# Score search ahead of the slot sums in every pair, and query weights three heads ahead

## The chip, the cores and the metric

The kernel runs on one core of a Trainium2 chip. The metric is the device time of one execution in microseconds, as the median of several runs. Names of engines in the profile: PE is TensorE's matmul, PEld its weight load, DVE is VectorE, ACT is ScalarE, POOL is GpSimd, SP is SyncE, which issues most of the DMAs.

## The reference

A normalised input `xn` of 2048 tokens by 512 feeds two branches, and both are added to `x`.

```python
xn = layernorm(x)
# A: attention, 32 heads of 16, one shared key and value head
p = softmax(q @ k.T * 16 ** -0.5); A = (p @ v) @ wo
# B: product-key experts, 32 heads, 64 x 64 = 4096 experts
s1 = q1 @ k1.T; s2 = q2 @ k2.T          # per head, 64 scores each
# two best of each, four candidate sums, the best two of them are the experts of the head
g = softmax(top_s)
act = gelu(xn . u[top_e]); B = sum(g * act * v[top_e])
out = x + A + B
```

So each token has 64 slots (32 heads, two experts), each with a row of `u`, a row of `v`, a gate and a gelu.

## The kernel before, in words

The tokens are four groups of 512, called phases 0 to 3, each of four tiles of 128 tokens. Phases 0 and 1 take part of the experts' work slot by slot; phases 2 and 3 do it densely over all 4096 experts, by one-hot matrices of gates. The 32 heads are 8 blocks `c` of four. The order of the score stages is `SEQ`: phase 0 with all blocks, phase 1 with two, phase 2 with all and its dense stage, phase 1 with the other six, phase 3 with all and its dense stage.

Everything after the start stands in a schedule written out by hand: a loop over `d`, 256 pairs of attention steps and some more at the end. `att_steps` (L1136) issues in each pair: score matmuls of one key block (`sc`, L326) with their exponentials on ScalarE (`pt`, L329), the `pv` matmuls of the pair before (L340), then `mid()`, the score matmuls of the next key block, a projection block if one is due (L433), and `fill()`. Score tiles for the exponentials have two PSUM buffers, `pv` one, and everything else (`psc`, `pw`, `pwt`, `pwo`, `pact`, `pout` and so on) shares three PSUM buffers with tag `x`.

`fill()` (L1313) runs `score_thread` by costs until the spent cost reaches an aim that grows evenly over the pairs, at most 4.0 a pair. The thread yields pieces of expert scores (`psc`, L531, 12 matmuls a tile), the making of the next block's combined weights (`wp_make`: `pw`, L486, `pwt`, L493, and the split of a weight tile into a high and a low part, L495 on ScalarE and L496 on VectorE), and the dense stages. When a score tile is complete, `item` (L512) searches it on VectorE: eight MAX8 (L544) and eight FIND_INDEX8 (L546). The search is what releases the PSUM buffer. After the fourth tile of a block `batch` (L563) does the index arithmetic (L571 to L632); the gates follow two pairs later, after an exponential on ScalarE (L583), in `gates` (L605 or L634).

`mid()` (L1258) does the slot work on VectorE. In order: tanhs of finished groups of four slots (L998, on ScalarE), then `dots` (L982, the product of a gathered row of `u` and the token), the slot weights (`w`, L1005), and then `go()` (L1288): sums `xa += w * v` (L1017), interleaved with `CHAIN`, the gelu polynomials of groups just completed (`gq`, `gy`, `ga`, L991 to L993), and with `rest`, the work held in `BEHIND`: gates, low parts of splits, and the sums of projection blocks (L437). It ends with up to four gathers on POOL (L970), which wait for the sums to free one of twelve buffers, and with stores of finished rows (L449). A group's tanh is issued in the `mid()` of the pair after its polynomial.

`dense_on` says which stage runs: 0 score tiles, 4 the last two score tiles of a dense phase, 2 the one-hot stage, 3 its end, 1 the dense sums. In stage 2 alone `go` is put into `POST_FILL`, which `fill()` runs at its end, and there the polynomials are issued in `mid()` directly after the dots.

The dense thread starts with `spread` (L749, `ptd` at L752): it transposes three tables. The third needs the last gates; until `gated_all` is set the thread gives the pair back without more work.

Query weights are loaded by `wp_load` (L465), 512 KB a head, on SP's queue, two heads ahead in buffers of tag `gy` (three of them, also used for gates in the dense stage). Tag `wd` has four buffers, used from the one-hot stage on.

Of the kernel before, what the change touches and what calls it, by code (L numbers as in the profile page):

```python
# [11 lines left out]
F32 = mybir.dt.float32  # L12
# [11 lines left out]
P = 128  # L24
S = 2048
D = 512
# [7 lines left out]
NC = 8  # L34
# [21 lines left out]
def tile_kernel(ctx, tc, x, wq, wkv, wo, wqT, kT, uv, ub, vb, out):  # L56
# [5 lines left out]
    late = [None]  # L62
# [383 lines left out]
    def experts_out(t):  # L446
        acc, last = ACC[t], t // GT == QB[3]
        assert last or t in DONE_A
        store(lambda: nc.sync.dma_start(d_part[t] if last else out[t * P:(t + 1) * P, :], acc))  # L449
        LIVE.discard(t)  # L450
# [14 lines left out]
    def wp_load(c, h):  # L465
        if late[0] is None or (c == 1 and h < 2):
            w = gtile(F32, (P, 2, D), "wqt") if c == 0 and h > 1 else big.tile([P, 2, D], F32, name="wqt", tag="wqt", bufs=2)
        else:
            w = late[0].tile([P, 2, D], F32, name="wqt", tag="gy", bufs=3)
        nc.sync.dma_start(w, wqT[4 * c + h].rearrange("(s p) d -> p s d", p=P))  # L470
        WC["raw", c, h] = w

    def wk_tile():
        return big.tile([P, 2, 512], F32R, name="wk", tag="wk", bufs=NWK)

    def wp_make(c):

        wt = [big.tile([P, 2, 512], F32, name="wt", tag="da", bufs=2) for _ in range(2)]
        for h in range(4):
            for n in range(4 * c + h + 1, min(4 * c + h + 3, 4 * NC) if late[0] else 4):  # L480
                if ("raw", n // 4, n % 4) not in WC:
                    wp_load(n // 4, n % 4)
            w = WC.pop(("raw", c, h))
            p = xtile("pw")
            for s in range(2):
                nc.tensor.matmul(p[s * E:(s + 1) * E, :], kTs[:, s, :], w[:, s, :], start=True, stop=True)  # L486
            nc.scalar.copy(wt[h // 2][:, h % 2, :], p)
            yield 0.9
        WC[c] = []
        for k in range(KC):  # L490
            p = xtile("pwt")
            for h in range(4):
                nc.tensor.transpose(p[:, h * P:(h + 1) * P], wt[h // 2][:, h % 2, k * P:(k + 1) * P], ident)  # L493
            wk = wk_tile()
            nc.scalar.copy(wk[:, 0, :], p)  # L495
            nc.vector.tensor_tensor(out=wk[:, 1, :], in0=p, in1=wk[:, 0, :], op=OP.subtract)  # L496
            WC[c].append(wk)
            store(lambda k=k, wk=wk: nc.sync.dma_start(d_w[c][:, k], raw(wk[:])))
            yield 0.45
# [501 lines left out]
    def weigh(n):  # L1001
        if n not in WT and n < a_ready[0] // SB:
            ga, th = GA.pop(n), TH.pop(n)
            w = small.tile([P, SB], F32, name="w", bufs=3)
            nc.vector.scalar_tensor_tensor(w, th, 1.0, ga, op0=OP.add, op1=OP.mult)  # L1005
            WT[n] = w
# [17 lines left out]
    def gathers(most):  # L1024
        while g_next[0] < NSL and g_next[0] < a_next[0] + NGB - lent[0] and most > 0:
            gather(g_next[0])
            g_next[0] += 1
            most -= 1

    def dots(to):  # L1030
        while d_next[0] < min(to, NSL):
            dot(d_next[0])
            d_next[0] += 1

    def adds(most):
        while a_next[0] < a_ready[0] and most > 0:
            add(a_next[0])
            a_next[0] += 1
            most -= 1

    def tanhs(to):
        while a_ready[0] + SB <= to:
            tanh(a_ready[0] // SB)
            a_ready[0] += SB
# [8 lines left out]
    def run(fns):  # L1053
        todo = fns[:]
        fns.clear()
        for fn in todo:
            fn()
# [6 lines left out]
    def flush():  # L1064
        posts()
        for _ in range(2):
            for fns in (ON_ACT, LAST, LATER, BEHIND):
                run(fns)
            ON_ACT.extend(LATER_ACT)
            LATER_ACT.clear()  # L1070
        run(ON_ACT)
        run(BEHIND)
# [40 lines left out]
    dense_on, quiet = [0], [0]  # L1113
# [3 lines left out]
    def run_scores(until=None, key=None):  # L1117
        while (until is not None and spent[0] < until) or (key is not None and key not in IDX):
            posts()
            try:  # L1120
                cost = next(sgen)
            except StopIteration:
                spent[0] = 1e9
                posts()
                return
            if cost is None:

                if key is None:
                    return
                continue  # L1130
            spent[0] += cost

    STEPS = 512


    def att_steps(d, mid, fill):  # L1136
        i = 2 * d
        run(STORES)
# [11 lines left out]
        if 0 < i <= STEPS:  # L1150
# [3 lines left out]
            if pk == 14:  # L1154
                unit_tail(pu)
        mid()
        if i < STEPS:
            scores(u, kc + 1, 0)
# [36 lines left out]
    for h in range(4):  # L1195
        wp_load(0, h)
# [8 lines left out]
    for i in range(2):  # L1205
        for k in range(2):
            w = start.tile([P, 2, 512], F32R, name="wqs", tag="wqs", bufs=4)
# [26 lines left out]
    run(STORES)  # L1234
    start_stack.close()
    wp_load(1, 0)
    wp_load(1, 1)
    late[0] = pool("late", bufs=1)
# [3 lines left out]
    with tc.manual_schedule(engines={E_.PE, E_.Activation, E_.DVE, E_.Pool, E_.SP}):  # L1242
        done0 = spent[0]
        half = STEPS // 2
        pos, since = 0.0, half
        for d in range(half + 24):


            if dense_on[0] != 0:
                since = d  # L1250
            if dense_on[0] == 1:
                pos += 2.6 if d < half * 3 // 4 else max(0.0, NSL - pos) / max(half - 3 - d, 1)
            else:
                pos += (2.1 if len(IDX) < NC * TPH else 2.3 if 0 <= d - since < 12 else 1.75, 0, 1.4, 1.5, 0.5)[dense_on[0]]

            todo = max(min(int(pos + 0.001), g_next[0]) - d_next[0], 0)

            def mid():  # L1258
                post = POST[:]
                POST.clear()  # L1260
                for act, _ in post:
                    act()
                tanhs(d_next[0])
                run(ON_ACT)
                ON_ACT.extend(LATER_ACT)
                LATER_ACT.clear()
                run(LAST)
                LAST.extend(LATER)
                LATER.clear()
                rest = BEHIND[:]  # L1270
                BEHIND.clear()

                dots(d_next[0] + todo - 1)
                if a_ready[0] > a_next[0]:
                    weigh(a_next[0] // SB)
                dots(d_next[0] + 1 if todo > 0 else 0)
                for _, fn in post:
                    fn()
                sums = min(a_ready[0] - a_next[0], max(todo, 3) if d < half else 4)
                if dense_on[0] > 2:  # L1280
                    sums = min(sums, 2)
                if quiet[0] > 0:
                    quiet[0] -= 1
                    sums = 0
                if dense_on[0] == 2:
                    run(CHAIN)

                def go():  # L1288
                    n = sums
                    while rest or CHAIN or n > 0:  # L1290
                        if n > 0:
                            adds(1)
                            n -= 1
                        elif not rest:
                            run(CHAIN)
                        if CHAIN:
                            CHAIN.pop(0)()
                        if rest:
                            rest.pop(0)()
                    gathers(4)  # L1300

                    for _ in range(1 if d < half - 4 else NT):
                        if OUTS:
                            experts_out(OUTS.pop(0))

                if dense_on[0] == 2:
                    POST_FILL.append(go)
                else:
                    go()

            aim = done0 + (FILL - done0) * (d + 1) / half if d < half else 1e6

            def fill():  # L1313
                run_scores(until=min(aim, spent[0] + MOST))
                run(POST_FILL)

            att_steps(d, mid, fill)
        flush()
        run(STORES)
        while a_next[0] < NSL:  # L1320
            dots(NSL)
            run(CHAIN)
            tanhs(d_next[0])
            adds(SB)
            run(STORES)
            gathers(NGB)
        assert not OUTS
        run(STORES)
# [37 lines left out]
```

## Time and profile before

| | |
|---|---|
| median of 3 runs | 1946.3 us (1936.64 to 1952.67) |
| profiled execution | 1941.6 us, span 1939.9 us |
| mean granted TensorE clock | 0.98 |
| score stages of phases 0, 1, 2 | about 145 to 611 us of the span |
| one-hot and dense stage of phase 2 | about 611 to 1085 us |
| the other score stages | about 1090 to 1437 us |
| one-hot and dense stage of phase 3 | about 1437 to 1908 us |

A row of the waits names who waited, its line, who ended the wait, the total, how often, and the longest. A row in order of time has start, length, engine, line, operation, tiles and count, and in brackets the idle time of the engine just before it and what ended it. "Busy" of PE counts pipelined matmuls with modelled ends.

### The profile page before, as it was taken

The numbers are of one execution on the slowest core, as the hardware profiler recorded it, in microseconds if no ns is written. First come the engines' busy times: TensorE is split into PE (matmuls) and PEld (weight loads), VectorE is DVE, ScalarE is ACT, GpSimd is POOL, SyncE is SP. The second block draws the span as 40 slices with busy tenths as digits, with TensorE's granted clock in tenths as the row PEclk, the third lists the DMA queues.
The fourth block names the chain that finished last, engine by engine and source line by source line (L and its number), as shares of the span: only waits on it lengthen the run. The fifth ranks groups of instructions, "written<-read, shape, count | busy, mean of one in ns | idle before, by whom it ended". The sixth has DMA issues, their size and how long they took to land.

```text
span 1939.9 us, 34783 instructions
## 1 busy us (share of the span) xinstructions
PE 1867.8 (96%) x10990; PEld 994.5 (51%) x10990; DVE 1674.6 (86%) x6717; ACT 1294.0 (67%) x1803; POOL 561.4 (29%) x536
## 2 busy tenths in 40 slices
PE   6879999999999999999999999999999999999998
PEld 4634444555554544555555445555555445555553
DVE  6627788999999986999999889999998779999994
ACT  3336666655556887777877555555578877788873
POOL 1202223222221222343444332222212124344430
PEclk9979999999998999999999999999998999999999
DMA  7857889787773667899899978877646788989882
GB/s 271 309 186 250 281 271 300 274 297 259 245 242 100 210 224 254 247 284 295 267 286 304 361 272 274 275 232 268 213 130 200 239 239 279 287 271 293 279 274 85
DMA packets 234393, 491.11 MB, mean 253 GB/s; under 512 B 93396, under 2 KB 93396, under 8 KB 234204
## 3 DMA queue, kind: packets, MB, share of 16 engines
q0 software_dynamic: 73728, 268.47, 41.8%
q1 hardware_dynamic: 159240, 219.56, 34.8%
q8 instruction: 88, 1.44, 0.3%
q10 hardware_dynamic: 1236, 0.82, 0.1%
q14 instruction: 101, 0.83, 0.1%
HBM read 427.41 MB, written 56.07 MB: 249 GB/s over the span
## 4 chain that ended last, share of the span: by engine, by line
PE 65%; DVE 21%; DMA 3%; ACT 2%; issue 2%; SPq 0%; ACTq 0%; DVEq 0%
PE pv L340 18%; PE sc L326 13%; PE psc L531 10%; PE pact L727 9%; PE pout L855 9%; DVE i L546 5%; DVE xa L1017 3%; DVE m L544 3%; DVE g L982 3%; PE pwo L433 2%; PE pg L809 2%; ACT pt L329 2%; PE pw L486 2%; DVE oh L777 1%; DMA rw<-in_ub_dram 1%
## 5 line engine op out<-in xcount | busy, mean ns | idle before, releaser
L329 ACT ACTIVATE pt<-sc 128x1024 f32<-128x1024 f32 x1024 | 993.4, 1026 | 453.5 <-PE sc L326 404.7
L970 POOL DMA_INDIRECT g<-in_uv_dram,idx x512 | 553.5, 1081 | 1324.5 <-DVE xa L1017 673.3
L340 PE MATMUL pv<-pt,vaug 128*32 128x512 f32 x4096 | 509.4, 615 | 0.0
L326 PE MATMUL sc<-qa,kaug 64*128 64x512 f32 x2048 | 387.7, 453 | 12.3 <-ACT pt L329 11.3
L531 PE MATMUL psc<-wk,xt 128*128 128x512 f32 x1536 | 388.6, 400 | 7.4 <-DVE wk L496 3.5
L1017 DVE SCALAR_TENSOR_TENSOR xa<-g,w,xa 128x512 f32<-128x512 f32 x512 | 372.2, 745 | 0.1
L982 DVE CUSTOM_DVE_ANT_0 g<-g,xa 128x512 f32<-128x512 f32 x512 | 335.5, 681 | 11.9 <-DMA g<-in_uv_dram,idx 11.9
L531 PEld LDWEIGHTS psc<-wk,xt 128*128 128x128 f32 x1536 | 277.6, 188 | 111.4 <-issue 40.2
L326 PEld LDWEIGHTS sc<-qa,kaug 64*128 64x128 f32 x2048 | 157.1, 186 | 334.2 <-ACT pt L329 206.0
L340 PEld LDWEIGHTS pv<-pt,vaug 128*32 128x32 f32 x4096 | 108.8, 111 | 253.7 <-issue 252.0
L546 DVE FIND_INDEX8 i<-m,psc 128x8 uint32<-128x64 f32 x1024 | 206.4, 221 | 0.0
L727 PE MATMUL pact<-xt,wk 128*128 128x512 f32 x768 | 197.5, 402 | 1.1 <-DVE i L546 1.1
L855 PE MATMUL pout<-wk,wd 128*128 128x512 f32 x768 | 194.9, 402 | 0.2 <-DVE wd L913 0.2
L727 PEld LDWEIGHTS pact<-xt,wk 128*128 128x128 f32 x768 | 140.1, 189 | 50.8 <-issue 18.2
L855 PEld LDWEIGHTS pout<-wk,wd 128*128 128x128 f32 x768 | 140.8, 188 | 47.4 <-DVE act L982 5.1
L544 DVE MAX8 m<-psc 128x8 f32<-128x64 f32 x1024 | 146.0, 214 | 19.3 <-PE psc L531 18.6
L692 DVE TENSOR_TENSOR wk<-rw,wk 128x512 fp32r<-128x512 f32 x128 | 84.8, 683 | 12.9 <-ACT wk L691 12.9
L858 DVE TENSOR_TENSOR da<-da,pout 128x512 f32<-128x512 f32 x128 | 82.7, 679 | 9.7 <-PE pout L855 9.6
L691 ACT CAST wk<-rw 128x512 fp32r<-128x512 f32 x128 | 73.9, 628 | 6.4 <-DMA rw<-in_ub_dram 6.4
L777 DVE TENSOR_TENSOR oh<-oh 128x2048 f16<-128x2048 f16 x64 | 78.0, 1219 | 0.0
L809 PEld LDWEIGHTS <-oh 128*128 128x128 f16 x1024 | 68.5, 163 | 14.5 <-issue 8.8
L809 PE MATMUL pg<-oh 128*128 128x32 f16 x1024 | 73.6, 247 | 1.9 <-DVE oh L780 1.9
(156 smaller groups left out, 1285.9 us busy)
## 6 DMA issues: line engine op xcount, KB each, us to landing
wk<-dw SPq DMA_DIRECT2D x96, 512.0 KB
wqt<-in_wqT_dram SPq DMA_DIRECT2D x32, 512.0 KB
dw<-wk SPq DMA_DIRECT2D x32, 512.0 KB
rw<-in_ub_dram SPq DMA_DIRECT2D x64, 256.0 KB
rw<-in_vb_dram SPq DMA_DIRECT2D x64, 256.0 KB
gy<-dg SPq DMA_DIRECT2D x64, 256.0 KB
qa<-dqh SPq DMA_DIRECT2D x128, 64.0 KB
g<-in_uv_dram,idx POOLq DMA_INDIRECT x512
```

The source lines that it names most:

```text
L326: nc.tensor.matmul(p[:, b, :], kaug[o:o + 64, kc * P:(kc + 1) * P], QA[u][o:o + 64, i, :], start=True, stop=True)
L329: nc.scalar.activation(pt, p, AF.Exp, scale=SCALE)
L340: nc.tensor.matmul(PV[u][32 * j:32 * j + 32, :], vaug[:, kc, :], pt[:, b, :], start=kc == 0, stop=kc == 15)
L531: nc.tensor.matmul(p, XT[g][k][:, a, j * P:(j + 1) * P], WC[n_][k][:, bb, :], start=n == 0, stop=n == 11)
L544: nc.vector.max(m8[:, jb, s, :], p[:, s * E:(s + 1) * E])
L546: nc.vector.max_index(i8[:, jb, s, :], m8[:, jb, s, :], p[:, s * E:(s + 1) * E])
L727: nc.tensor.matmul(p, us[:, a, k * P:(k + 1) * P], XT[DG][k][:, c, :], start=n == 0, stop=n == 11)
L809: nc.tensor.matmul(p[:, i * NB:(i + 1) * NB], oa[:, :, i], ob[:, :, i], start=True, stop=True)
L855: nc.tensor.matmul(p, wd[0][:, a, j * P:(j + 1) * P], vs[:, c, :], start=n == 0, stop=n == 5)
L970: nc.gpsimd.indirect_dma_start(out=gt, out_offset=None, in_=uv, in_offset=bass.IndirectOffsetOnAxis(ap=IDX[ph, c, ti][:, s:s + 1], axis=0))
L982: nc.vector.tensor_tensor_reduce(u, u, XN[TPH * ph + ti], scale=1.0, scalar=0.0, op0=OP.mult, op1=OP.add, accum_out=a[:, i:i + 1])
L1017: nc.vector.scalar_tensor_tensor(acc, v, w[:, i:i + 1], acc, op0=OP.mult, op1=OP.add)
```

## The change

`go` is put behind the fill in stages 0 and 4 as well as in 2. The stage that issues the polynomials directly after the dots is still stage 2 alone. The query weights take the buffers of tag `wd` and are loaded up to three heads ahead.

```diff
@@ wp_load
         else:
-            w = late[0].tile([P, 2, D], F32, name="wqt", tag="gy", bufs=3)
+            w = late[0].tile([P, 2, D], F32, name="wqt", tag="wd", bufs=4)
@@ wp_make
         for h in range(4):
-            for n in range(4 * c + h + 1, min(4 * c + h + 3, 4 * NC) if late[0] else 4):
+            for n in range(4 * c + h + 1, min(4 * c + h + 4, 4 * NC) if late[0] else 4):
                 if ("raw", n // 4, n % 4) not in WC:
                     wp_load(n // 4, n % 4)
@@ mid
-                if dense_on[0] == 2:
+                if dense_on[0] in (0, 2, 4):
                     POST_FILL.append(go)
                 else:
                     go()
```

## The prediction

> **What bounds the kernel now.** I read the page's first part, then busy time by stretches, then the waits inside the stretches that the change touches, then single pairs in order of time. All sums stand against the profiled execution: 1941.6 us, with a span of 1939.9. The median of the timed runs is 4.7 above it, and those runs lie 16 apart.
>
> ```profile
> span 1939.9 us, 34783 instructions
> PE 1867.8 (96%) x10990; PEld 994.5 (51%) x10990; DVE 1674.6 (86%) x6717; ACT 1294.0 (67%) x1803; POOL 561.4 (29%) x536
> ```
>
> PE, the TensorE, is busy all but 72 us. So the whole can shrink only by PE's idle time and by time lost to a lower clock, and it can grow by anything that makes PE wait. The next rows are the four stretches in which score tiles are searched (window, length, then PE, PEld, DVE, ACT and POOL busy, granted clock, DMA share, GB/s).
>
> ```profile
> 145.00:440.00 295.00, 284.97 (x1640) 140.97 (x1644) 250.17 (x1398) 188.42 (x247) 79.70 (x79) 1.00 0.81 280
> 440.00:611.00 171.00, 166.40 (x948) 91.72 (x941) 167.10 (x1103) 99.27 (x123) 41.06 (x41) 1.00 0.67 220
> ...
> 1090.00:1300.00 210.00, 207.47 (x1153) 110.07 (x1153) 190.69 (x1171) 119.45 (x146) 59.86 (x60) 1.00 0.80 274
> 1300.00:1437.00 137.00, 132.51 (x769) 73.41 (x765) 132.66 (x848) 80.39 (x103) 34.94 (x34) 1.00 0.65 215
> ```
>
> PE's idle time is 10.0, 4.6, 2.5 and 4.5 us, 21.6 together: that is all that a better order can win inside them. VectorE (DVE) idles 45, 3.9, 19 and 4.3. So there are two kinds of stretch. In the first and third PE leads and VectorE has room. In the second and fourth both are full: there VectorE's own work sets the pace as much as PE's, and no order of the same work shortens it. Who ends PE's waits, by stretch (waiter, line, releaser, us in total, times, longest): first 145 to 440, then 440 to 611, then 1300 to 1440.
>
> ```profile
> PE psc L531 <- DVE wk L496: 3.5, 4, 1.6
> PE pwt L493 <- DVE i L546: 2.3, 1, 2.3
> PE pw L486 <- DMA wqt<-in_wqT_dram: 1.8, 1, 1.8
> PE pw L486 <- issue: 1.1, 1, 1.1
> ```
>
> ```profile
> ACT gth L998 <- DVE gy L992: 4.6, 3, 2.9
> PE ptd L752 <- DVE da L643: 2.7, 1, 2.7
> ```
>
> ```profile
> PE psc L531 <- DVE i L546: 1.6, 1, 1.6
> PE ptd L752 <- DVE da L643: 1.4, 1, 1.4
> PE pact L727 <- DVE i L546: 0.9, 1, 0.9
> ```
>
> **The change, part by part.** No instruction is added or removed; VectorE gets another order, and one 512 KB load per head goes out a head earlier. Until now a pair's VectorE work ran dots, slot sums with gelu polynomials and gates, then the search of the score tile. Now it runs dots, search, sums.
>
> *Query weights.* The third load ahead needs a fourth buffer; it takes the tag of four that stands idle until the one-hot stage, so nothing else waits for it. On SyncE's queue one load moves up past a store of the weight tiles.
>
> ```profile
> 223.39 9.63 DMA wqt<-in_wqT_dram
> ...
> DVE w L1005 <- ACT gth L998: 51.0, 39, 4.3
> DVE g L982 <- DMA g<-in_uv_dram,idx: 11.9, 7, 4.4
> ```
>
> The first row is of the chain of waits, the others of the waits of the whole run. The chain holds one such load, 9.63 us long, and PE waited for it 1.8 us. A head is over once per pair or slower, so one more head ahead covers it. I also credit the 1.1 of line 486 that no releaser is named for. Worth 0 to 2.9; I take 2.5.
>
> *Search first, in 145 to 440.* The splits of the next weight tiles (L496) and the release of PSUM (L546) now stand ahead of two or three sums. The wait of 2.3 at L493 and the three shorter ones of the four at L496 (3.5 less its longest, 1.6, which I leave standing) are covered by that: 2.3 + 1.9 = 4.2, of which I take 3.5.
>
> *What the move makes late.* The gelu polynomial (gq, gy, ga) now stands behind the search too, and the tanh that reads gy stands in ScalarE's queue in the next pair, between the exponentials. Those feed PE. The search of one tile, in the chain of waits:
>
> ```profile
> 476.20 1.05 DVE m L544 x8
> 477.25 1.60 DVE i L546 x8
> ```
>
> That is 2.65 us. Every fourth tile brings the index arithmetic, from L571 to L632 in order of time, and the same view shows where gy, the tanh and the next exponential stand:
>
> ```profile
> 471.21 0.17 DVE L571 TENSOR_TENSOR s<-m 128x16 f32<-128x16 f32 x1
> ...
> 474.13 0.18 DVE L632 SCALAR_TENSOR_TENSOR da<-hi,ii 128x32 f32<-128x32 f32 x1
> ...
> 483.81 0.16 DVE L992 SCALAR_TENSOR_TENSOR gy<-gq,act 128x4 f32<-128x4 f32 x1
> ...
> 484.45 0.21 ACT L998 ACTIVATE gth<-gy 128x4 f32<-128x4 f32 x1
> 485.13 1.94 ACT L329 ACTIVATE pt<-sc 128x1024 f32<-128x1024 f32 x2 [0.48 <-PE sc L326]
> ```
>
> The arithmetic takes 3.1 us. The tanh follows gy by 0.48 us (484.45 less 483.97), so there is no reserve at this place: gy moves 2.65 later with one search, 5.3 with two, 5.75 with one and the arithmetic, 8.4 with two and it. How late may a tanh be before PE feels it? The trace of before has one case:
>
> ```profile
> 564.10 0.21 ACT L998 ACTIVATE gth<-gy 128x4 f32<-128x4 f32 x1 [2.87 <-DVE gy L992]
> ...
> 566.29 0.50 PE L326 MATMUL sc<-qa,kaug 64*128 64x512 f32 x2 [0.29 <-ACT pt L329]
> ```
>
> A tanh 2.87 late cost PE 0.29, so about 2.6 is free. In the first stretch gy stands several us ahead of its tanh:
>
> ```profile
> 180.53 0.16 DVE L992 SCALAR_TENSOR_TENSOR gy<-gq,act 128x4 f32<-128x4 f32 x1
> ...
> 185.00 0.21 ACT L998 ACTIVATE gth<-gy 128x4 f32<-128x4 f32 x1
> ```
>
>  In the built order of the changed kernel ten groups of four slots lie in 440 to 611: three move by one search, two by two, three by one and the arithmetic, two by two and the arithmetic. The first excess makes PE wait, and this wait brings VectorE nearer to PE for all that follows, so it isn't paid again by each group: the largest, 8.4 less 0.5 and 2.6 plus what the trace is already late there, leaves some 7 us of PE waits in all. By the same count 1300 to 1437 gets 6. In 145 to 440 the 4.3 us of reserve covers one search, and I allow 1 for the groups with more.
>
> Are those 7 and 6 lost? VectorE's work in these stretches is unchanged and fills 98% and 97%, so PE's waits only come earlier than they did, unless VectorE idles. It can: where PE is held back, the search meets a tile that isn't complete, and the sums that used to fill such a time stand behind it. Below, none; above, the whole 7 and 6. Nearest are the 3.9 and 4.3 that it idles there now; I take 3 more in each.
>
> *The way into the one-hot stage.* The last gates now run behind the fill, so the pair that waited for them in the fill is left without filler and the gates are read one pair later. The built order shows it: the score and pv matmuls of one attention pair now stand between the second and the third spread of the tables. In order of time, an attention pair and that place:
>
> ```profile
> 601.31 0.73 PE L326 MATMUL sc<-qa,kaug 64*128 64x512 f32 x4
> 601.97 1.92 PE L340 MATMUL pv<-pt,vaug 128*32 128x512 f32 x16
> 603.82 0.73 PE L326 MATMUL sc<-qa,kaug 64*128 64x512 f32 x4
> ...
> 607.30 0.66 PE L752 MATMUL ptd<-ident,da 128*128 128x128 f32 x4 [0.68 <-ACT oh L753]
> 610.69 1.12 PE L752 MATMUL ptd<-ident,da 128*128 128x128 f32 x4 [2.73 <-DVE da L643]
> ```
>
> An attention pair is 3.4 us of PE work (0.73 + 1.92 + 0.73), and it now fills the wait of 2.73. That balances the 3 in the first full stretch; in the fourth stretch the wait at L643 was 1.4 and those at L546 1.6 and 0.9, 3.9 together, against 3. I count both as 0.
>
> *Other queues.* Adds release the gather buffers, so POOL issues each gather 2.65 to 5.75 later; gathers were waited for seven times, 11.9 in all. Between nothing and seven more searches, 18.6; VectorE has 19 of idle time where they lie, so I take 1. A projection sum (L437, eight in all) now also stands behind a search and holds a PSUM bank for as long: nothing to eight searches, 21; half of them lie in dense stages, where nothing moves, so I take 0.5. SyncE stores of finished rows go out a few places later; nobody waits for them.
>
> Sum: -2.5 - 3.5 + 1 + 0 + 0 + 1 + 0.5 = **-3.5**, or 1938 on the profiled run and 1943 on the median; I say 1941.
>
> **A rule beside the rows.** Past the wait at L643 the clock fell:
>
> ```profile
> 605.00:611.00 6.00, 2.06 (x12) 1.16 (x12) 5.72 (x21) 2.66 (x4) 3.08 (x3) 0.95 0.41 97
> ...
> 617.00:645.00 28.00, 27.95 (x224) 13.36 (x222) 26.63 (x55) 21.06 (x36) 2.37 (x2) 0.76 0.37 116
> 645.00:700.00 55.00, 53.53 (x536) 29.95 (x532) 50.57 (x103) 48.55 (x80) 14.63 (x12) 1.00 0.68 225
> ...
> 1443.00:1478.00 35.00, 35.00 (x298) 16.82 (x290) 30.39 (x64) 27.18 (x47) 6.59 (x6) 0.80 0.52 165
> ```
>
> PE was busy 2.06 of 6 us, and then ran 28 us at 0.76 before the same work got a clock of 1.00; the second time it was 35 us at 0.80. That is 6.7 and 7.0 us of lost clock. The Trainium skill, "TensorE: Matmul & The Clock Gate", section "What's actually happening", has the half clock come after an idle window of about 3.4 us. The trace agrees in kind; by that rule my longest added wait would bring a low clock of its own. The skill's "PSUM — Partial Sum Buffer", section "Engine vs sequencer instructions", calls ScalarE's queue strict FIFO, which speaks against putting gy behind a search; the tanh of 564.10, which held the exponentials behind it, agrees.
>
> **Rivals.** *The tanh holds PE (slower).* If VectorE doesn't absorb PE's waits, the 7 and 6 count in full, with 3 in the two other stretches, and one more low-clock spell of some 7 us at each of the two full stretches: 16 + 14 - 6 = 24, that is 1966 on the profiled run. It decides from the point where a tanh comes over 2.6 late more than once per stretch. For it: the reserve of 0.48. Against: VectorE was the full engine there anyway. Another cost of the same place: w (L1005) already waits 51 us for tanhs, and now has one dot instead of a search between gy and itself. *The clock stays up (faster).* If the pair that fills the wait keeps PE at work, the 6.7 and 7.0 go: 1938 - 14 = 1924. Against: the one-hot stage has small matmuls, and the clock may fall whatever comes before. *Nothing shows.* The loads and the splits were hidden often enough, the order averages out: 1941 to 1943, hardly to be told from the forecast.
>
> **How the numbers follow.** Forecast 0.40, nothing shows 0.17, tanh 0.28, clock 0.15. This kernel can be told from no change from about 1% on, 19 us. The forecast and the second rival lie within it; the tanh rival lies beyond it in most of its reach, and I add a little for the gathers (18.6): slower 0.29. The clock rival passes 1% only with nearly all of PE's idle time too: faster 0.13. Same 0.58. The range goes from 1920 (clock rival, and a third of the idle 21.6) to 1966.
>
> **What would show it.** Right: the waits at L493, L486 and L643 gone, PE idle 145 to 440 near 5; tanh waiting for gy well over its 4.6 in 440 to 611 while that stretch keeps its length plus one pair. Wrong: these stretches some 10 us longer with PE waiting for pt; or a one-hot stage at clock 1.00 from its start.

## The result, and the profile after

The changed kernel takes **1961.3 us** as the median of six runs (1956.6 to 1966.0), against 1947.2 for the kernel before, beside it. The ratio is **1.0077, 95% interval 1.0060 to 1.0094**: some 14 us slower, where 3.5 us faster was forecast. The value lies inside the range 1920 to 1966, near its upper end, and the sign is wrong. The profiled execution of the kernel after took 1956.6 us, the lowest of its six, and that of before 1941.6, also below its median: the two spans lie 15.0 us apart, about as far as the medians (14.1).

The head of the page, with the groups of the exponentials' scores and of the tanh (busy us, mean ns, idle time before it and who ended most of it):

```profile
span 1954.9 us, 34837 instructions
PE 1871.4 (96%) x10990; PEld 994.6 (51%) x10990; DVE 1675.6 (86%) x6717; ACT 1293.1 (66%) x1803; POOL 571.4 (29%) x536
L326 PE MATMUL sc<-qa,kaug 64*128 64x512 f32 x2048 | 392.8, 456 | 22.8 <-ACT pt L329 21.5
L998 ACT ACTIVATE gth<-gy 128x4 f32<-128x4 f32 x128 | 26.9, 210 | 85.8 <-DVE gy L992 80.8
```

The work is the same (10990 matmuls, VectorE busy for 1675.6 us). PE's idle time, span less busy time, went from 72.1 to 83.5 us, and its busy time up by 3.6. So 11.4 of the 15.0 us are new waits. The same windows as before the change:

```profile
145.00:440.00 295.00, 286.65 (x1652) 141.01 (x1652) 250.88 (x1425) 189.12 (x247) 80.12 (x76) 1.00 0.82 277
440.00:611.00 171.00, 163.59 (x915) 90.60 (x913) 162.70 (x1064) 92.64 (x115) 43.64 (x40) 0.99 0.66 217
...
1300.00:1450.00 150.00, 145.22 (x826) 79.49 (x824) 141.71 (x923) 86.77 (x110) 36.07 (x34) 1.00 0.64 210
```

In the first window PE does 1.7 us more than before; in the second it does 2.8 us less, and VectorE 4.4 us less. The waits, first of 145 to 440, then of 440 to 611, then of 1300 to 1450:

```profile
ACT gth L998 <- DVE gy L992: 14.4, 8, 3.6
DVE w L1005 <- ACT gth L998: 8.1, 4, 3.5
PE psc L531 <- DVE wk L496: 3.5, 4, 1.6
PE pwt L493 <- DVE i L546: 1.1, 1, 1.1
```

```profile
ACT gth L998 <- DVE gy L992: 31.7, 9, 6.3
PE sc L326 <- ACT pt L329: 6.9, 9, 2.5
```

```profile
ACT gth L998 <- DVE gy L992: 22.2, 7, 4.5
PE sc L326 <- ACT pt L329: 4.6, 8, 1.3
```

ScalarE stands at the tanh for 31.7 us where it stood 4.6, and PE's scores wait for exponentials (pt) 6.9 us. The same view of before, 440 to 611, has for these scores:

```profile
PE sc L326 <- ACT pt L329: 0.3, 1, 0.3
```

The longest case in the kernel after, in order of time:

```profile
583.08 0.75 DVE L1017 SCALAR_TENSOR_TENSOR xa<-g,w,xa 128x512 f32<-128x512 f32 x1
583.93 0.16 DVE L992 SCALAR_TENSOR_TENSOR gy<-gq,act 128x4 f32<-128x4 f32 x1
584.13 0.20 ACT L998 ACTIVATE gth<-gy 128x4 f32<-128x4 f32 x1 [6.32 <-DVE gy L992]
584.24 2.83 ACT L329 ACTIVATE pt<-sc 128x1024 f32<-128x1024 f32 x3
585.30 0.62 PE L326 MATMUL sc<-qa,kaug 64*128 64x512 f32 x2 [2.47 <-ACT pt L329]
```

The tanh waits 6.32 us for gy; the exponentials, whose scores have been ready since 578.5, start behind it, and the next score matmuls stand 2.47 us until the first of them has read its bank.

Where the 15.0 us arise is seen best by the start of the same matmul in both traces. The table gives lengths between such starts: tile 4 is the first of a score tile's matmuls (L531) at 151.75 us, tiles 40 to 71 are phase 2, 96 to 127 phase 3. "Before, again" is a second profile of the unchanged kernel, told of below.

| stretch | before | after less before | before, again, less before |
|---|---|---|---|
| start to tile 4 | 151.8 | -1.0 | -1.0 |
| tile 4 to 40 (slots picked) | 275.5 | **-2.4** | 0.0 |
| tile 40 to 43 | 15.0 | +1.5 | +1.4 |
| tile 43 to 71 (phase 2) | 148.8 | **+8.7** | 0.0 |
| tile 71 to the one-hot matmuls (L809) | 26.5 | -3.4 | +0.7 |
| one-hot stage to the first dense sum (L855) | 144.6 | +1.8 | +2.5 |
| dense sums, to tile 72 | 323.9 | **+5.1** | 0.0 |
| tile 72 to 85 (slots picked) | 99.0 | -2.4 | -1.2 |
| tile 85 to 100 | 82.6 | +2.3 | 0.0 |
| tile 100 to the second one-hot stage (phase 3) | 167.2 | **+6.2** | +0.1 |
| second one-hot stage | 141.7 | -1.3 | +1.3 |
| second dense stage, to the end | 363.2 | -0.2 | -0.3 |

Phase 2's score tiles cost 8.7 - 3.4 = 5.3 us until the one-hot stage starts and phase 3's 6.2; the dense sums lose 5.1. Of what the change gains, 2.4 are left in the first stretch. The 6.2 are not all loss: between tile 100 and the first one-hot matmul of phase 3 the kernel after has one attention pair more (8 score and 16 pv matmuls, some 3.4 us of work), which in before stands behind the first 16 one-hot matmuls. Measured to the first score matmul behind 32 one-hot matmuls, where both have done the same work, phase 3 costs 4.1. What the dense sums waited for, in two views of 760 to 1090 us of the kernel after:

```profile
DVE gy L898 <- DMA gy<-dg: 7.2, 2, 5.5
DVE rc L378 <- DMA rc<-dsum: 3.3, 1, 3.3
```

```profile
PE pout L855 <- DVE wd L913: 2.8, 1, 2.8
PE pout L855 <- DVE gy L898: 1.4, 1, 1.4
```

VectorE stands at a reciprocal whose 16 KB have not landed; behind it stand a product with the gates and its low part (`wd`), and PE waits for that. In the same views of before VectorE waits 1.9 us for gy and not at L378, and PE not at L855.

### The profile page after: what moved, and what is told of

It reads as the page before. It is cut to its first block, busy times and chain, and to the rows that moved or that the text cites. A ratio compares the mean times of both kernels' runs of the same rounds, so it can differ in the third digit from the quotient of the medians.

```text
span 1954.9 us, 34837 instructions
## 1 busy us (share of the span) xinstructions
PE 1871.4 (96%) x10990; PEld 994.6 (51%) x10990; DVE 1675.6 (86%) x6717; ACT 1293.1 (66%) x1803; POOL 571.4 (29%) x536
## 4 chain that ended last, share of the span: by engine, by line
PE 62%; DVE 19%; DMA 6%; ACT 4%; issue 2%; SPq 1%; DVEq 0%; ACTq 0%
PE pv L340 18%; PE sc L326 13%; PE psc L531 9%; PE pout L855 8%; PE pact L727 8%; DVE i L546 5%; DVE m L544 3%; DVE xa L1017 3%; PE pg L809 3%; ACT pt L329 3%; DVE g L982 2%; PE pwo L433 2%; PE pw L486 1%; DMA gy<-dg 1%; DMA dg<-gst 1%
## 5 line engine op out<-in xcount | busy, mean ns | idle before, releaser
L329 ACT ACTIVATE pt<-sc 128x1024 f32<-128x1024 f32 x1024 | 992.3, 1025 | 409.1 <-PE sc L326 363.2
L970 POOL DMA_INDIRECT g<-in_uv_dram,idx x512 | 563.5, 1101 | 1329.6 <-DVE xa L1017 701.2
L326 PE MATMUL sc<-qa,kaug 64*128 64x512 f32 x2048 | 392.8, 456 | 22.8 <-ACT pt L329 21.5
L531 PE MATMUL psc<-wk,xt 128*128 128x512 f32 x1536 | 388.6, 400 | 5.4 <-DVE wk L496 3.5
L531 PEld LDWEIGHTS psc<-wk,xt 128*128 128x128 f32 x1536 | 277.6, 188 | 109.5 <-issue 41.2
L855 PE MATMUL pout<-wk,wd 128*128 128x512 f32 x768 | 195.2, 402 | 5.9 <-DVE wd L913 3.0
L855 PEld LDWEIGHTS pout<-wk,wd 128*128 128x128 f32 x768 | 140.7, 188 | 53.8 <-issue 5.1
L998 ACT ACTIVATE gth<-gy 128x4 f32<-128x4 f32 x128 | 26.9, 210 | 85.8 <-DVE gy L992 80.8
L809 PE MATMUL pg<-oh 128*128 128x32 f16 x1024 | 73.6, 246 | 7.1 <-DVE oh L780 7.1
L809 PEld LDWEIGHTS <-oh 128*128 128x128 f16 x1024 | 68.4, 163 | 19.8 <-issue 10.9
```

Of the source, the lines that this page charges most:

```text
L326: nc.tensor.matmul(p[:, b, :], kaug[o:o + 64, kc * P:(kc + 1) * P], QA[u][o:o + 64, i, :], start=True, stop=True)
L329: nc.scalar.activation(pt, p, AF.Exp, scale=SCALE)
L531: nc.tensor.matmul(p, XT[g][k][:, a, j * P:(j + 1) * P], WC[n_][k][:, bb, :], start=n == 0, stop=n == 11)
L809: nc.tensor.matmul(p[:, i * NB:(i + 1) * NB], oa[:, :, i], ob[:, :, i], start=True, stop=True)
L855: nc.tensor.matmul(p, wd[0][:, a, j * P:(j + 1) * P], vs[:, c, :], start=n == 0, stop=n == 5)
L970: nc.gpsimd.indirect_dma_start(out=gt, out_offset=None, in_=uv, in_offset=bass.IndirectOffsetOnAxis(ap=IDX[ph, c, ti][:, s:s + 1], axis=0))
```

## The experiments

All kernels compute the whole of the reference. Ratios are to the kernel before, run beside each, with 95% intervals. A length "by the starts" is a row of the table above, measured in that kernel's own trace and given as the difference to before.

### The parts alone

*The loads alone*: the new order taken back.

```diff
-                if dense_on[0] in (0, 2, 4):
+                if dense_on[0] == 2:
                     POST_FILL.append(go)
```

> The query weights three heads ahead, nothing else. Theory A (the loss of the change is the gelu polynomials standing behind the search, and the loads are harmless): 1 to 3 us below the kernel before, with the PE wait of 1.8 us for a query-weight load gone. Theory B (the loads disturb other transfers of the first 440 us or the dense stages): at least 3 us above before.

Measured: 1946.3 us, ratio **1.0003 (0.9980 to 1.0026)**. PE's waits in 145 to 440:

```profile
PE psc L531 <- DVE wk L496: 3.5, 4, 1.6
PE pwt L493 <- DVE i L546: 2.3, 1, 2.3
PE sc L326 <- ACT pt L329: 1.4, 2, 1.0
PE pw L486 <- issue: 1.0, 1, 1.0
PE psc L531 <- DMA xt<-dxt: 1.0, 1, 1.0
```

The wait for a query weight is gone, the 1.0 of L486 without a releaser stays. From tile 4 to 40 nothing is won (+0.8): PE waits 0.9 us less, but behind the wait of 2.3 its clock is halved for 3.4 us (315.9 to 319.3), which costs 1.7. In the timed runs the loads neither help nor hurt as far as can be told: the interval goes from 4 us below to 5 above, so the 1 to 3 below of theory A are not excluded.

*The order alone*: the query weights as before.

```diff
-            w = late[0].tile([P, 2, D], F32, name="wqt", tag="wd", bufs=4)
+            w = late[0].tile([P, 2, D], F32, name="wqt", tag="gy", bufs=3)
...
-            for n in range(4 * c + h + 1, min(4 * c + h + 4, 4 * NC) if late[0] else 4):
+            for n in range(4 * c + h + 1, min(4 * c + h + 3, 4 * NC) if late[0] else 4):
```

> Sums, polynomials and gates behind the search, loads as before. Theory A: the whole loss and a little more, 15 to 18 us above before, with tanhs waiting for gy some 30 us in 440 to 611. Theory B: less than 10 us above before, the rest being the loads' doing.

Measured: 1960.3 us, ratio **1.0073 (1.0047 to 1.0099)**, the whole loss. By the starts -2.5 to tile 40, +10.4 from tile 43 to 71, -3.3 behind it, +5.8 in the dense sums, +6.1 from tile 100. So the 2.4 us won in the kernel after are the order's too. PE has no wait for a query weight from 145 to 440 in this run either, though it loads them as before; nor has it in the run with the polynomial alone, below.

*The polynomial taken out of the move*: gq, gy, ga directly behind the dots in all stages, sums and gates still behind the search.

```diff
-                if dense_on[0] == 2:
+                if dense_on[0] in (0, 2, 4):
                     run(CHAIN)
```

> The changed kernel with one more edit: in score stages too the gelu polynomials are issued directly after the dots, so only sums and gates stand behind the search. Theory A (the late tanh is the cause): the 9 us lost in 440 to 611 and the 4 lost in 1300 to 1437 come back, total 0 to 6 us below before. Rival C (not the tanh but sums and gates behind the search make it slower, through gates, gather buffers or VectorE waiting for incomplete tiles): still 8 to 15 us above before.

Measured: 1948.8 us, ratio **1.0010 (0.9990 to 1.0030)**. In 440 to 611:

```profile
ACT gth L998 <- DVE gq L991: 4.1, 1, 4.1
ACT gth L998 <- DVE gy L992: 2.4, 4, 1.1
PE sc L326 <- ACT pt L329: 1.5, 2, 1.0
```

Three instructions of 0.16 us each per group, put ahead of the search, take away most of the loss. By the starts: +3.1 from tile 43 to 71, then -5.2, a net gain of 2.1 until the one-hot stage. Theory A has the mechanism; that the run is 0 to 6 us below before, as it says too, is not shown.

*The polynomial alone moved*: the kernel before, with only gq, gy, ga behind the search.

```diff
                 if dense_on[0] == 2:
                     run(CHAIN)
+                elif dense_on[0] in (0, 4):
+                    polynomials = CHAIN[:]
+                    CHAIN.clear()
+                    POST_FILL.append(lambda: [fn() for fn in polynomials])
```

> The kernel before with only the gelu polynomials put behind the search in score stages; sums and gates stay ahead of it, loads as before. Theory A: it has the loss by itself, 10 to 18 us above before. Rival C: within 4 us of before, since sums and gates are where they were.

Measured: 1952.0 us, ratio **1.0031 (1.0014 to 1.0047)**. In 440 to 611:

```profile
ACT gth L998 <- DVE gy L992: 28.8, 9, 6.3
PE sc L326 <- ACT pt L329: 6.4, 8, 2.4
```

The same waits as in the kernel after, from the polynomial alone, and by the starts +8.2 from tile 43 to 71 and -4.2 behind it. This is the cause in phase 2's tiles, produced and removed. But the whole run has only some 40% of the loss, between the two expectations: from tile 100 on it loses 1.3 instead of 6.2 (or of 4.1 at the same work), and nothing in the dense sums.

*The slot sums alone moved*: the run with the polynomial first, with the gates ahead of the search as well.

```diff
                     run(CHAIN)
+                if dense_on[0] in (0, 4):
+                    run(rest)
```

> The kernel after, with polynomials and gates (the products with the up gate and the inverse sums) in the first and last score tiles ahead of the search, and only the slot sums behind it. Theory that the late polynomial is what costs: tanh waits for gy in 440 to 611 as little as in the run with the polynomial first (2.4 us), time within 4 us of it, 1945 to 1952. Rival, sums behind the search cost by themselves (a search starts no earlier, and the gathers behind the sums come late): 1953 to 1960.

Measured: 1946.1 us, ratio **1.0023 (1.0005 to 1.0042)**; tanh waits for gy 6.0 in 440 to 611, PE for pt 0.4. By the starts -2.6 to tile 40, +0.9 and +0.1 in phase 2. The sums can stand behind the search at a cost at the limit of what is measured, and the gain to tile 40 comes from them.

### The stages apart

*The order in the slot-picking tiles only, and in phases 2 and 3 only.* A flag, set per block of heads, tells which tiles are under way.

```diff
         for n, (ph, c) in enumerate(SEQ):
+            gathered[0] = ph < NSP
...
-                if dense_on[0] in (0, 2, 4):
+                if dense_on[0] == 2 or dense_on[0] == 0 and gathered[0]:
                     POST_FILL.append(go)
```

> The kernel after, with the new order only while the score tiles are those that pick slots to gather (to about 425 us, and from 1086 to about 1250), where TensorE used to wait for VectorE's search; the old order in the score tiles of the dense phases (425 to 611 and 1250 to 1450). Theory that the loss is made in the dense phases' score tiles, where TensorE waits for exponentials, while the search ahead is a true gain in the others: 3 to 4 us ahead of the kernel before at tile 40, kept past 611, no more than 1 us lost from tile 43 to tile 71, time 1938 to 1945. Rival, the order costs wherever it comes, by gathers and loads that bunch: what is won by tile 40 is lost in the transfers after 1086, time 1948 to 1956.

The second kernel has `dense_on[0] in (2, 4) or dense_on[0] == 0 and not gathered[0]` there.

> The kernel after, with the new order only in the score tiles of the dense phases (425 to 611 and 1250 to 1450) and the old one in the others. Theory that the loss is made there: 7 to 10 us lost from tile 43 to tile 71, time 1956 to 1962, as slow as the kernel after or 3 us slower. Rival, it needs the lateness of the tiles before: no more than 3 us lost there, time 1945 to 1952.

Measured: slot-picking tiles 1950.4 us, ratio **1.0029 (1.0009 to 1.0049)**; phases 2 and 3 1963.9 us, ratio **1.0117 (1.0087 to 1.0148)**. The second in 440 to 611:

```profile
ACT gth L998 <- DVE gy L992: 31.7, 9, 6.3
PE sc L326 <- ACT pt L329: 6.8, 8, 2.5
```

The loss is made in the tiles of phases 2 and 3: +7.4 and -3.3 in phase 2, +7.8 from tile 100 (5.7 at the same work). It needs nothing of what stands before; the time lies 2 us above the theory's range. This run loses another 6.3 from tile 72 to 85, where its order is the old one and PE waits 4.7 us for wk<-dw. The first kernel gains 2.5 to tile 40 and loses 0.9 from 43 to 71, as the first theory has it, yet its time misses that theory's 1938 to 1945 and lies in the rival's range: from tile 85 to 100 it loses 4.8.

*The order in the first 40 tiles only.*

```diff
-            gathered[0] = ph < NSP
+            gathered[0] = n < 10
```

> The run with the new order in the slot-picking tiles alone, with that order now only in the first 40 tiles (to about 425 us), and the old one from 1086 on. Theory that the search ahead wins some 3 us there and that the second group of such tiles (where TensorE's starts fell back 4.8 us from tile 85 to tile 100) loses it: from tile 4 to tile 40 the starts gain 2.5 to 3.5 us on the kernel before, from tile 85 to tile 100 they lose under 1 us, and the time is 1940 to 1945, 0 to 4 us below the kernel before. Rival, the loss from 1190 to 1250 is in the transfers and not in this order: the same fall-back of over 3 us there, time 1948 to 1952 as in that run.

Measured: 1943.2 us beside 1942.0, ratio **1.0000 (0.9977 to 1.0022)**. By the starts -2.4 from tile 4 to 40 and 0.0 from tile 85 to 100: the 4.8 were this order's. At tile 127 this trace is still 2.8 us ahead, but its second one-hot stage is 5.1 longer. In the timed runs no gain shows, though the time lies in the 1940 to 1945 that were forecast. No kernel of the study beats the kernel before.

*The order without the last two tiles of each dense phase.*

```diff
-                if dense_on[0] in (0, 2, 4):
+                if dense_on[0] in (0, 2):
```

> The kernel after, with the new order in the first score tiles alone and not in the last ones (1300 to 1450). Theory that late exponentials are lost time wherever they come: the last tiles give back the 4 to 5 us that the kernel after lost from tile 100 to the start of the second one-hot stage, time about 1956 (1954 to 1958). Rival, an early pause of TensorE there is given back by a higher granted clock in the one-hot stage behind it: time unchanged within 2 us of the kernel after, about 1961.

Measured: 1957.4 us, ratio **1.0065 (1.0039 to 1.0091)**. The expectation was put wrongly: stage 4 is only the last two tiles of a phase, so most of 1250 to 1450 kept the new order, and tanh still waits for gy 21.3 us from 1300 on. So the run doesn't test its theory, and its trace is that of the slowest of six executions (1965.2 us). It is of use in another way: in phase 2's tiles its order is that of the kernel after but for the last two, and it repeats the loss there (+10.2, then -5.6).

### What the late instructions meet

*The tanh a pair later.* ScalarE's queue is spared the wait in another way: a group's tanh is issued a pair later, gy stays behind the search.

```diff
+        d_before = [0]
...
-                tanhs(d_next[0])
+                tanhs(d_before[0] if dense_on[0] in (0, 4) else d_next[0])
+                d_before[0] = d_next[0]
```

> The kernel after, with the tanh of a block of slots issued one attention pair later in the score tiles, so that ScalarE no longer stands at it; gates and sums stay behind the search. Theory of the tanh that holds ScalarE's queue: in 440 to 611 tanh waits for gy under 10 us in all (31.7 in the kernel after), TensorE's scores wait for pt under 2 us (6.9 there), the loss from tile 43 to tile 71 falls from 8.8 us to under 3, and the time is about 1951 (1947 to 1955): what is left is the dense stage's 5 us. Rival, VectorE itself is the bound there (the order costs it time): ScalarE's wait goes and the stretch keeps its length, time 1958 to 1963.

Measured: 1960.9 us, ratio **1.0090 (1.0056 to 1.0124)**. In 440 to 611 the theory's sizes hold: tanh waits for gy 3.9, PE for pt 1.4, +0.9 from tile 43 to 71, then -2.3. But the run is not faster: its time lies in the rival's range, though the stretch did not keep its length as the rival has it. PE waits for transfers, first in 425 to 450, then in 1090 to 1300:

```profile
PE psc L531 <- DMA xt<-dxt: 3.0, 1, 3.0
```

```profile
PE psc L531 <- DMA wk<-dw: 4.0, 2, 3.0
```

By the starts +4.8 from tile 40 to 43 and +6.3 from 72 to 85. So the mechanism is confirmed in its place, and the forecast of the whole (about 1951) is wrong. The slots' weights, sums and gathers come a pair later too, but that this is the price is not shown: from tile 72 to 85 the run with phases 2 and 3 only loses 6.3 and the one with the polynomial first 4.9, with the same wait for wk<-dw (4.7 and 4.2 us) and no later tanh.

*The reciprocal two steps later*, to let its load land.

```diff
-            if r == 6:
+            if r == 8:
                 pair_invert(pp - 1)
-            if r == 10:
+            if r == 12:
                 pair_spread(pp - 1)
-            if r == 12:
+            if r == 14:
                 pair_tail(pp - 1)
```

> The kernel after, with the reciprocal of a pair's sums, the load of its inverse and the product behind it issued two steps later, behind the same load. Theory that the dense stage's loss at about 1080 us is VectorE standing at L378 until the load rc<-dsum has landed: that wait (3.3 us) and TensorE's wait for the gate product behind it (2.8 us) go, and the time is 3 to 5 us below the kernel after, about 1957. Rival, the wait is only where a shifted phase of the stage's transfers shows: another wait takes its place and the time stays within 2 us of the kernel after, about 1961.

Measured: 1971.0 us, ratio **1.0145 (1.0119 to 1.0170)**, 10 us slower than the kernel after. VectorE's wait at L378 is gone from 760 to 1090, but its wait for gates is still 7.2 there, and behind that stage stands a new one:

```profile
DVE gy L898 <- DMA gy<-dg: 7.2, 2, 5.8
```

```profile
PE psc L531 <- DMA wk<-dw: 6.3, 1, 6.3
```

The dense sums lose 7.6 by the starts and tile 72 to 85 another 7.6. Both texts of the expectation miss; the rival's idea, that another transfer takes the place, is nearer. Why it costs 10 us more was not settled; the trace, that of the slowest of six executions (1981.0 us), loses 11.8 from tile 43 to 71 and 11.0 from tile 100 as well.

*The kernel before, once more*, for a second profile.

> The kernel before, unchanged, for a second profile of it. Theory that the waits are fixed by the order of the instructions and the granted clock alone changes from execution to execution: TensorE's starts agree with the first profile within 2 us up to tile 71, and its idle time (72.1 us in the first) within 3 us, while the span differs by the clock in the one-hot stages. Rival, transfers land differently each time: idle time differs by over 5 us, and differences between single profiles of 5 us mean nothing.

```profile
span 1943.2 us, 34783 instructions
PE 1870.4 (96%) x10990; PEld 994.5 (51%) x10990; DVE 1676.3 (86%) x6717; ACT 1295.0 (67%) x1803; POOL 563.6 (29%) x536
```

PE's idle time is 72.8 against 72.1, and the lengths agree within 0.1 us in the score tiles 4 to 40, 43 to 71 and from 85 on. The two one-hot stages differ, by 2.5 and 1.3 us, and tiles 40 to 43 and 72 to 85 by 1.4 and 1.2. So a difference of 5 us between single traces in phase 2's tiles is real. In a one-hot stage even 5 us say nothing: the first one is 5.1 longer with the loads alone, whose order there is that of before.

### The rows that decide

Differences to before by the starts, in us; the fourth column is the sum of the two ahead of it. The last one measures from tile 100 to the first score matmul behind 32 one-hot matmuls, where all kernels have done the same work.

| kernel | tile 4 to 40 | 43 to 71 | 71 to one-hot | phase 2's tiles | dense sums | 72 to 85 | 85 to 100 | 100 to one-hot | 100 to the same work |
|---|---|---|---|---|---|---|---|---|---|
| after | -2.4 | +8.7 | -3.4 | +5.3 | +5.1 | -2.4 | +2.3 | +6.2 | +4.1 |
| order alone | -2.5 | +10.4 | -3.3 | +7.1 | +5.8 | -2.3 | +2.0 | +6.1 | +4.0 |
| reciprocal later | -2.1 | +11.8 | -4.0 | +7.8 | +7.6 | +7.6 | +1.8 | +11.0 | +8.9 |
| phases 2 and 3 only | +0.3 | +7.4 | -3.3 | +4.1 | +0.4 | +6.3 | -0.2 | +7.8 | +5.7 |
| without last two tiles | -2.5 | +10.2 | -5.6 | +4.6 | 0.0 | -0.1 | +4.7 | +3.4 | +3.4 |
| polynomial alone | +1.4 | +8.2 | -4.2 | +4.0 | 0.0 | -0.9 | +1.8 | +1.3 | +1.3 |
| polynomial first | -2.6 | +3.1 | -5.2 | -2.1 | -0.1 | +4.9 | +0.8 | +3.3 | +1.2 |
| slot sums alone | -2.6 | +0.9 | +0.1 | +1.0 | +0.5 | +0.5 | 0.0 | +1.0 | +1.0 |
| tanh a pair later | +1.6 | +0.9 | -2.3 | -1.4 | -0.1 | +6.3 | +0.6 | +2.1 | 0.0 |
| slot-picking tiles only | -2.5 | +0.9 | -0.3 | +0.6 | 0.0 | -0.5 | +4.8 | -0.1 | -0.2 |
| first 40 tiles only | -2.4 | +0.7 | +0.3 | +1.0 | 0.0 | -1.5 | 0.0 | -0.4 | -0.5 |
| loads alone | +0.8 | 0.0 | +0.6 | +0.6 | 0.0 | -1.2 | 0.0 | 0.0 | 0.0 |

In these rows, whenever tanh has to wait for a gy behind the search in phase 2, its tiles cost 4 to 8 us; whenever it does not, they cost -2 to +1. In phase 3, at the same work, the first six kernels of the table cost 1.3 to 8.9 and the others -0.5 to +1.2. There the polynomial alone costs 1.3 and the rest of the order without it 1.2, together less than the 4.1 of the kernel after: in phase 3 the polynomial is not shown to be the main cause. The 5 us in the dense sums come in the kernel after, with the order alone and with the reciprocal later; the run without the last two tiles, with the same order in all the tiles before them, doesn't have them, nor does the order in phases 2 and 3 only. What brings them stays open, and so do the 5 to 8 us from tile 72 to 85, which come and go with no order that the rows show. So only phase 2's 5.3 have a cause that was both produced and removed. The losses in the dense sums and in phase 3 all but go when the polynomial is put first (-0.1 and +1.2), but moving it alone doesn't bring them (0.0 and +1.3).

## Why the prediction was wrong

**Query weights, -2.5 forecast, 0 measured.** The wait for the load went, but it also went in two runs that load as before (order alone, polynomial alone), so that it went by the earlier load is not shown. The 1.0 of L486 that I credited stayed, and a wait for xt of 1.0 came, as it did in the second profile of before (1.1). Order with loads and order without them gain the same to tile 40, 2.4 and 2.5. The term was mis-sized by all of itself.

**Search first and late tanh in 145 to 440, -3.5 + 1 forecast, -2.4 measured.** The net is right by luck. Of the waits, that at L493 fell from 2.3 to 1.1 instead of going, and the 3.5 at L496, of which 1.9 were to go, did not move; most of the rest of the gain is the 1.8 of the query weight, which I had put down to the loads. That w waits 8.1 for its tanh, half of before's 16.7 in this window, costs or saves VectorE only, which has room there.

**Phase 2's and phase 3's tiles, 0 and 0 forecast, +5.3 and +6.2 measured (4.1 at the same work).** This is the step that failed. The count of late groups gave 7 us of PE waits for 440 to 611 and 6 for 1300 on; the traces have 6.9 and 4.6, so the mechanism was right. That the 7 fits so well is in part luck: the working shows 8.4 - 0.5 - 2.6 = 5.3 of it and no figure for the rest, and it has one wait that is paid once, where the trace has nine, the longest 2.5. What was wrong is what I made of them: "VectorE's work in these stretches is unchanged and fills 98% and 97%, so PE's waits only come earlier than they did", less 3 us of idling that the extra attention pair should balance. The busy time between the starts of tiles 43 and 71, before and after, shows what happened (window, length, PE, PEld, DVE, ACT, POOL, clock, DMA share, GB/s):

```profile
442.32:591.16 148.84, 148.40 (x842) 82.77 (x841) 145.64 (x962) 85.70 (x105) 36.39 (x36) 1.00 0.72 236
```

```profile
440.46:598.03 157.57, 150.90 (x842) 83.72 (x841) 152.45 (x988) 85.64 (x105) 43.64 (x40) 0.99 0.70 232
```

PE was busy for 148.40 of 148.84 us: in this stretch it was PE that set the length, and VectorE ran behind it with a reserve in the buffers. Held back by exponentials, PE needs 157.57 for the same 842 matmuls: it waits 6.7 us instead of 0.4, and is busy 2.5 longer, of which 1.7 go to a halved clock shown below. VectorE idles only 1.9 us more (5.1 against 3.2); in the longer time it does 6.8 us of work that used to come behind tile 71. Behind tile 71 it has that much less to do, PE's waits for its tables (L643) are gone, and 3.4 us are given back, which is the sense in which a wait "comes earlier"; the remaining 5.3 are lost. From 98% I had read that VectorE sets the pace, though PE stood at 97% in the same window, and its one long wait, at L643, ended in the last microsecond of it.

**The extra attention pair.** The waits of PE for ptd, 3.9 in all between 605 and 630, are gone, but that the pair filled them is not shown. With the polynomial alone moved, or without the last two tiles, no pair stands between the spreads, and yet only 0.6 and 0.7 us are left of those waits: it is enough that PE comes late. Where the pair stands there, it is missing behind the spreads, and the one-hot matmuls wait:

```profile
PE pg L809 <- DVE oh L780: 3.4, 2, 2.0
PE sc L326 <- ACT pt L329: 0.7, 2, 0.5
```

3.4 for 3.9: nothing was left of it to balance the 3. The two runs without the pair have no such wait. In phase 3 the 3.9 that I set against the other 3 did go, but there too PE waits anew: 4.6 us for exponentials and 1.4 at L809.

**Gathers, +1; projection sums, +0.5.** VectorE's waits for gathers did not grow: 11.9 us before, 3.5 after, and 4.4 more for which no releaser is named. The new waits are for other transfers and in another stage, the 5.1 of the dense sums (rc<-dsum, gy<-dg). No term stood for that. From tile 85 to 100 the order costs 1.8 to 4.8 us in the five runs that have it there whole, and -0.2 and 0.0 in the two that leave it out there; no term stood for that either, and only part of it is found: in the run with slot-picking tiles alone, with its 4.8, PE waits 2.6 us for tanh and exponentials in 1190 to 1300.

**The rivals.** *The tanh holds PE* had the mechanism and the sign, with a chance of 0.28. Its price of 24 us was too high: the two full stretches cost 5.3 and 4.1 instead of 7 and 6 with a low-clock spell of 7 each. A low clock did come, but shorter: behind the longest wait it was halved for 3.4 us, 1.7 lost (the wait's stretch and the next; the granted clock stands third from the end):

```profile
582.10:585.50 3.40, 0.93 (x6) 0.45 (x4) 2.81 (x16) 1.37 (x3) 0.94 (x1) 1.00 0.01 2
585.50:588.90 3.40, 3.10 (x16) 0.88 (x18) 3.40 (x26) 3.37 (x5) 0.00 (x0) 0.50 0.55 154
```

The order alone has two such stretches between tiles 43 and 71, phases 2 and 3 only has none, and that is most of what sets their +10.4 and +7.4 apart. In the fourteen traces together, by their clock records and matmuls, every one of the 13 stretches of 3.4 us in score tiles in which PE was busy for less than 40% was followed by a halved clock, and none of some 2900 in which it was busy for over 90%.

*The clock stays up* falls in both directions. In the six microseconds whose idle time had preceded the low clock PE was now busy, and the clock was low all the same:

```profile
605.00:611.00 6.00, 5.26 (x33) 2.89 (x31) 2.96 (x17) 3.92 (x7) 0.00 (x0) 1.00 0.00 0
...
617.00:645.00 28.00, 24.54 (x186) 12.25 (x185) 19.84 (x39) 18.05 (x32) 0.19 (x1) 0.76 0.35 110
645.00:700.00 55.00, 53.37 (x526) 29.59 (x526) 51.62 (x106) 48.41 (x80) 11.14 (x10) 0.97 0.63 203
```

0.76 as before, with PE busy for 5.26 us of the six in question. The idle time now lies in waits of at most 2.0 us at 621 and 624. The 0.76 is a mean; the clock goes to and fro between half and whole:

```profile
623.10:629.90 6.80, 5.59 (x36) 2.19 (x36) 6.70 (x15) 2.48 (x4) 0.00 (x0) 0.50 0.03 6
629.90:633.30 3.40, 3.40 (x44) 2.69 (x40) 3.37 (x7) 2.48 (x4) 0.00 (x0) 1.00 0.00 0
633.30:636.70 3.40, 3.40 (x20) 0.59 (x16) 3.26 (x10) 3.00 (x5) 0.00 (x0) 0.50 0.03 6
```

The Trainium skill, "TensorE: Matmul & The Clock Gate", section "What's actually happening", has the half clock after an idle window of about 3.4 us and the full one after as long a busy one. The trace agrees with the length of the stretches but not with the condition: 2.47 us of waiting were enough at 585.5, and at 633.3 the clock is halved behind 3.40 us in which PE shows as busy all the time. Idle time does not explain that one.

**What the clock adds.** Over the 80 timed runs of the kernel before the mean granted clock lies between 0.973 and 0.986, 0.9787 on average, and a thousandth of it goes with 1.4 us (the 29 runs from 0.980 up average 1939.1 us, the 14 up to 0.976 average 1948.0). The six runs of the kernel after average 0.9750. By that slope 3.7 thousandths are 5 us, about a third of the loss. The five other kernels whose medians lie 14 us or more above before average 0.973 to 0.976, the rest 0.9775 to 0.980. In the score tiles the stretches above show the direction: first the wait, then the halved clock. Most halved stretches lie in the one-hot stages, though, many behind stretches in which PE was busy throughout, so how much of the 5 us the waits bring stays open.

## What to carry to other kernels

In a ring of engines (PE's scores, ScalarE's exponentials, VectorE's polynomials) a small instruction in an in-order queue sets the pace of all that stands behind it: before a block of work is moved, look for the one short producer in it that another engine waits for, and leave that producer in front. An engine that is busy for 97% and one that is busy for 98% of a stretch don't share the blame by rank: compare busy time between the starts of the same instructions, and see which of them has a reserve in buffers. A wait that is only shifted must show up as time given back in the next stretch; look for it there before counting it as nothing, and compare two kernels only between points ahead of which both have done the same work.

## What the runs showed of the hardware

Two profiles of the same kernel agreed within 0.1 us over three score stretches of 149 to 276 us, while the one-hot stages, with their small matmuls, varied by 1 to 2.5 us with the granted clock, which goes there between 0.50 and 1.00 in stretches of 3.4 us; over all kernels the second one-hot stage took from 138.0 to 148.3 us. In score tiles a halved clock followed where waits left PE busy for under 40% of such a stretch (0.93 of 3.40 us in the kernel after). PE's wait for a transfer (wk<-dw) from 1086 to 1100 was 2.1 us in one profile of the kernel before and 0.9 in the other: where transfers fill a stage (DMA share 0.90 in 760 to 1090), their landing isn't fixed by the program alone.
